# Three of wo's blocks loaded in mid-run, eight partitions a transfer, and the queries made after the turning

## The chip, the cores and the metric

The kernel runs on one core of one Trainium2 chip (trn2). The metric is device time in microseconds (us) of one execution. A kernel is run several times on the same chip; the number given is the median with the lowest and the highest. One more execution is taken with the hardware profiler. It has a time of its own, and inside that a span from the first to the last recorded instruction.

The engines are TensorE (PE for its matmuls, PEld for its weight loads), VectorE (DVE), ScalarE (ACT), GpSimd (POOL) and SyncE (SP). SP does no arithmetic here; it issues nearly all transfers, in program order, and an issue that waits holds up all issues behind it. Transfers are carried out by sixteen DMA engines.

## The reference

One decoding step of a block with two parallel branches on the same normalized input, in float32: grouped-query attention over a cache, and a dense layer with the Mish activation.

```python
B, Sq, D = 8, 1, 512
Hq, Hkv, Sk, Dh = 32, 8, 8192, 128
F = 1792
...
q = (xn @ wq).reshape(B, Sq, Hq, Dh)
k = repeat(k_cache, 4); v = repeat(v_cache, 4)
p = softmax(q @ k.T * Dh**-0.5)
A = (p @ v).reshape(B, Sq, Hq * Dh) @ wo
...
h = xn @ w1 + b1
act = h * tanh(softplus(h))
out = x + A + act @ w2
```

The caches hold 8 x 8 x 8192 x 128 numbers each, 268 MB. wq and wo have 8.4 MB each, w1 and w2 3.7 MB each. Every byte is read once.

## The kernel before, in words

The attention is cut into 32 units (`UNITS`). Unit j treats one batch b = j mod 8 and one pair of key heads m = j div 8, so eight query heads. Its keys are one transfer of 8.39 MB, its values another, each 64 KB in each of the 128 partitions (`load_unit`, L119 to L127). Both land in the one large tile `kv`: values always in the first 64 KB of a partition, keys by turns in two places that overlap by half.

A unit's work is written out by hand in the loop of L441 to L472. TensorE multiplies the unit's keys with the key weights in two halves (`scores`). Between the halves SP issues the keys of unit j + 1, which waits until the first half has read its place. `softmax` takes the maximum and the exponentials, into tile `e`. Then come the values of the unit *before* (`values`, 64 matmuls into bank O, and four VectorE operations that pick the wanted rows into `os`). Only then SP issues the values of unit j, since the place is free, and VectorE makes the next key weights. `turn` brings the unit's exponentials into the layout in which they multiply values: eight matmuls with permutations into X, the sum of the exponentials into M, its reciprocal, four transposes and two long reductions on VectorE. `merge` finishes the unit before: it turns `os` by one matmul into M, scales it with the reciprocal, and writes a column set of `oT[:, m]`.

Three times, for the pairs m = 1 to 3, the queries are made during the loop. At b = 4 SP issues a quarter of wq into `ws` (2 MB). At b = 5 `project` multiplies it: twice four matmuls into bank H, a copy by ScalarE into a tile named `e`, four matmuls into M, and at the end a scaled copy to `qT` by VectorE. In the kernel before it stands between `values` and `turn` (L466, L467). At b = 7 `spread` uses `qT`. The last wq goes through `ws` in units 20 and 21; after that `ws` is idle.

The end: wo comes as four transfers of 2 MB (L475 to L480) into the place of the values, each with four blocks of 512 KB, block u holding the rows of two query heads. w2 follows in three parts (L484 to L487) in the second half of the last keys' place. `outputs` multiplies `oT[:, m]` with its four blocks, eight matmuls for each m, four of them side by side on four groups of output columns; the sums stand in the first bank of X. They are copied to `a_sb`, and `down` adds the Mish branch with w2 and these sums into bank H. The result is H plus x.

Tiles of the pool `work` have two buffers unless a number is given; `e`, `os` and `a_sb` are of this kind. The Mish branch's activations are made in unit 0.

Of the kernel before, what the change touches and what calls it, by code (L numbers as in the profile page):

```python
# [8 lines left out]
F32 = mybir.dt.float32  # L9
# [4 lines left out]
P = 128  # L14
B = 8
D = 512
HKV = 8
REP = 4
DH = 128
# [8 lines left out]
BW = 1024  # L28
CC = D // P
# [3 lines left out]
Q = P // G  # L33
# [15 lines left out]
NJ = PL * HALF  # L49

W2R = 7

# [11 lines left out]
def kernel(  # L66
# [12 lines left out]
    nc = tc.nc  # L79
    PSUM = bass.MemoryType.PSUM  # L80

    const = ctx.enter_context(tc.tile_pool(name="const", bufs=1))
    work = ctx.enter_context(tc.tile_pool(name="work", bufs=2))
# [24 lines left out]
    xres = const.tile([P, P], F32, name="xres")  # L108
    oT = const.tile([P, NP, H2, B], F32, name="oT")
    aT = const.tile([P, 2 * W2R, B], F32, name="aT")  # L110
    pt8 = const.tile([P, HALF, PL * TL, H2], F32, name="pt8")
    tr = const.tile([P, PL * TL, 32], F32, name="tr")

    def load_q(m):

        rows = wq.rearrange("j p f -> (j p f)").rearrange("(m p f) -> m p f", m=NP, p=P)
        nc.sync.dma_start(ws, rows[m])
# [74 lines left out]
    for g in range(G):  # L192
# [4 lines left out]
            start=True,  # L197
# [15 lines left out]
    def project():  # L213

        w = ws.rearrange("p (c f) -> p c f", c=CC)
        for d in range(2):
            for c in range(CC):
                nc.tensor.matmul(  # L218
                    H[Q * c : Q * c + B, :],
                    xn4[:, c, :],  # L220
                    w[:, c, d * 512 : (d + 1) * 512],
                    start=True,
                    stop=True,
                )
            qp = work.tile([P, 512], F32, name="e")
            nc.scalar.copy(qp, H)
            for h in range(REP):
                at = 192 + (d * REP + h) * B
                nc.tensor.matmul(  # L229
                    M[:, at : at + B],  # L230
                    qp[:, h * DH : (h + 1) * DH],
                    bsel[:, :B],
                    start=True,
                    stop=True,
                )
        qT = work.tile([P, H2 * B], F32, name="qT", bufs=1)
        nc.vector.tensor_scalar_mul(qT, M[:, 192 : 192 + H2 * B], DH**-0.5)
        return qT
# [50 lines left out]
    def softmax(j):  # L289
        nm = work.tile([P, 1], F32, name="nm")  # L290
        nc.vector.tensor_reduce(nm, S, axis=AX.X, op=ALU.max, negate=True)  # L291
        nc.tensor.transpose(M[:1, 0:P], nm, ident)  # L292
        nr = work.tile([1, 2, REP], F32, name="nr")
        row = M[:1, 0:P].rearrange("p (c d k h) -> p d h c k", c=2, d=2, h=REP)
        for d in range(2):
            nc.vector.tensor_reduce(nr[:, d], row[:, d], axis=AX.XY, op=ALU.min)
        nx = work.tile([1, 2, 2, NH * G, REP], F32, name="nx", bufs=1)
        for c in range(2):
            nc.vector.tensor_copy(  # L299
                nx[:, c],  # L300
                nr.rearrange("p d (o h) -> p d o h", o=1).to_broadcast([1, 2, NH * G, REP]),
            )
        nc.tensor.transpose(  # L303
            M[:, 128:129], nx.rearrange("p c d k h -> p (c d k h)"), ident[:1, :1]
        )
        nmx = work.tile([P, 1], F32, name="nmx")
        nc.vector.tensor_copy(nmx, M[:, 128:129])  # L307
        e = E[j] = work.tile([P, 512], F32, name="e")
        l = work.tile([P, 1], F32, name="l")
        nc.scalar.activation(e, S, AF.Exp, bias=nmx, accum_out=l)  # L310
        lsel = work.tile([P, H2], F32, name="lsel")
        nc.vector.tensor_scalar(lsel, rsel, l, None, op0=ALU.mult)  # L312
        return lsel

    def turn(j, lsel):
        e = E.pop(j)
        for g in range(4):
            nc.tensor.matmul(X[:, g], perm[:, g], e, start=True, stop=True)  # L318
        nc.tensor.matmul(M[:, 136 : 136 + H2], ones, lsel, start=True, stop=True)  # L319
        RT[j] = work.tile([P, H2], F32, name="rt", bufs=3)  # L320
        nc.vector.reciprocal(RT[j], M[:, 136 : 136 + H2])  # L321
        for tl in range(TL):
            nc.vector.transpose(  # L323
                tr.rearrange("p (l t) c -> p t l c", t=TL)[:, tl],
                X.rearrange("p g (t q l) -> p t l g q", t=TL, q=PP)[:, tl],
            )
        for d in range(2):
            half = slice(64 * d, 64 * (d + 1))
            nc.vector.tensor_reduce(  # L329
                pt8[half, :, :, d * REP : (d + 1) * REP].rearrange("p c y h -> p y c h"),  # L330
                tr[half].rearrange("p y (g c h) -> p y c h g", g=4, c=HALF),
                axis=AX.X,
                op=ALU.add,
            )


    def values(j, vt):
        for n in range(NJ):
            l, c = divmod(n, HALF)
            q = n % G  # L340
            nc.tensor.matmul(  # L341
                O[Q * q : Q * (q + 1), :],
                pt8[:, c, TL * l : TL * (l + 1), :].rearrange("p t h -> p (t h)"),
                vt[:, 512 * n : 512 * (n + 1)],
                start=(n < G),
                stop=(n >= NJ - G),
            )
        os = work.tile([P, DH], F32, name="os")
        nc.vector.tensor_scalar(os, O[:, :DH], isel[:, 0:1], None, op0=ALU.mult)  # L349
        for i in range(1, TL):  # L350
            nc.vector.scalar_tensor_tensor(  # L351
                os, O[:, DH * i : DH * (i + 1)], isel[:, i : i + 1], os, op0=ALU.mult, op1=ALU.add
            )
        return os
# [49 lines left out]
        nc.vector.tensor_copy(aT, turned.rearrange("p (j q) -> p j q", q=Q)[:, :, :B])  # L404


    A = X[:, 0]

    def outputs(m, t):
        w = t.rearrange("p (u f) -> p u f", u=4)  # L410
        for d in range(2):
            for h in range(REP):
                nc.tensor.matmul(
                    A[Q * h : Q * h + B, :],
                    oT[:, m, d * REP + h, :],
                    w[:, d * 2 + h // 2, h % 2 * D : (h % 2 + 1) * D],
                    start=(m == 0 and d == 0),
                    stop=(m == NP - 1 and d == 1),
                )

    def down(lo, hi, w):
        for j in range(2 * lo, 2 * hi):
            for g in range(G):
                at = (j - 2 * lo) * D + g * P
                nc.tensor.matmul(  # L425
                    H[Q * g : Q * g + B, :P],
                    aT[:, j, :],
                    w[:, at : at + P],
                    start=(j == 0),
                    stop=(j == 2 * W2R - 1),  # L430
                )
# [9 lines left out]
    for j in range(UNITS):  # L441
        b = j % B
        more = j // B + 1 < NP

        k = k_t.pop(j)
        scores(j, k, j % 2 == 1, 0)
        if j == UNITS - 1:
            v_t[j] = load_unit(v, j, K_AT[0])
        elif j > 0:
            k_t[j + 1] = load_unit(kT, j + 1, K_AT[(j + 1) % 2])  # L450
        scores(j, k, j % 2 == 0, 1)
        WK.pop(j)
        lsel = softmax(j)
        os = None
        if j > 0:
            os = values(j - 1, v_t.pop(j - 1))
        if j + 1 < UNITS:
            v_t[j] = load_unit(v, j, V_AT)
            if more and b == SPREAD_Q:
                spread(qT)  # L460
            key_weights(j + 1)
        if j == 0:
            mish(w1_t, b1_sb, kv[:, W1_AT : W1_AT + 6 * FG])
        if more and b == LOAD_Q:
            load_q(j // B + 1)
        if more and b == MAKE_Q:  # L466
            qT = project()  # L467
        turn(j, lsel)
        if j > 0:
            merge(j - 1, os)  # L470
        if more and b == SPREAD_Q - 1:
            selections()  # L472


    w_o = [kv[:, 4096 * m : 4096 * (m + 1)] for m in range(NP)]  # L475
    for m in range(NP):
        nc.sync.dma_start(
            w_o[m].rearrange("p (u f) -> p u f", u=4),
            wo[4 * m : 4 * (m + 1)].rearrange("u p f -> p u f"),
        )  # L480
    w2_rows = w2.rearrange("j p f -> (j p) f").rearrange("(q i) f -> q (i f)", i=W2R)
    w2_t = []
# [8 lines left out]
        outputs(m, w_o[m])  # L491
    merge(UNITS - 1, os)
    outputs(NP - 1, w_o[NP - 1])
    a_sb = work.tile([P, 512], F32, name="e")
    nc.scalar.copy(a_sb, A)
    down(*parts[0], w2_t[0])
    for g in range(G):
        nc.tensor.matmul(
            H[Q * g : Q * g + B, :P],
            bsel[:, :B],  # L500
            a_sb[:, g * P : (g + 1) * P],
            start=False,
            stop=False,
        )
    for p, t in zip(parts[1:], w2_t[1:]):
        down(*p, t)
    res = work.tile([P, DH], F32, name="os")
    nc.vector.tensor_add(res, H[:, :P], xres)
    nc.sync.dma_start(out, res)


# [36 lines left out]
```

## Time and profile before

| | us |
|---|---|
| median of 3 runs | 1313.02 |
| lowest and highest | 1312.48, 1313.17 |
| the profiled execution | 1313.46 |
| its span | 1311.7 |
| PE busy (matmuls), share of the span | 985.5, 75% |
| DVE busy | 515.0, 39% |
| ACT busy | 40.2, 3% |
| granted TensorE clock, mean | 0.877 of full |

The whole program of an execution is one stream of instructions for each engine. The profile gives for each group of like instructions how often it ran, the busy time and mean, and the idle time of the engine ahead of it with what ended it. The chain of waits is followed back from the last instruction. A row of it has a start, a duration, and the engine and line, or the transfer, that set the end of that piece. A row of a stretch has the busy time of each engine in it, the granted clock, the share of the time in which the sixteen DMA engines carried packets (1.00 is all sixteen), and the rate. A share of 0.50 can mean eight engines busy all the time. The share is credited to the stretch in which a packet stands, so short stretches can be slightly above 1. The queue q1 is SP's, q10 ScalarE's, q8 and q14 carry instructions.

### The profile page before, as it was taken

The numbers are of one execution on the slowest core, as the hardware profiler recorded it, in microseconds if no ns is written. First come the engines' busy times: TensorE is split into PE (matmuls) and PEld (weight loads), VectorE is DVE, ScalarE is ACT, GpSimd is POOL, SyncE is SP. The second block draws the span as 40 slices with busy tenths as digits, with TensorE's granted clock in tenths as the row PEclk, the third lists the DMA queues.
The fourth block names the chain that finished last, engine by engine and source line by source line (L and its number), as shares of the span: only waits on it lengthen the run. The fifth ranks groups of instructions, "written<-read, shape, count | busy, mean of one in ns | idle before, by whom it ended". The sixth has DMA issues, their size and how long they took to land.

```text
span 1311.7 us, 11148 instructions
## 1 busy us (share of the span) xinstructions
PE 985.5 (75%) x5040; PEld 341.1 (26%) x5040; DVE 515.0 (39%) x728; ACT 40.2 (3%) x88; POOL 2.2 (0%) x9
## 2 busy tenths in 40 slices
PE   5968877768877668777878777687687678677666
PEld 3322222222322222222322222232232222222222
DVE  3463344432444442334243344414444432344431
ACT  1000000000000000000000000000000000000000
POOL 0000000000000000000000000000000000000000
PEclk9989888888888888887888788788898888888898
DMA  9999999999999999999999999999999999999997
GB/s 393 450 422 439 428 434 431 430 444 428 432 432 434 428 440 424 440 426 434 432 428 446 416 442 430 430 440 422 438 430 436 430 430 432 436 424 438 426 418 313
DMA packets 13591, 561.79 MB, mean 428 GB/s; under 512 B 1244, under 2 KB 1376, under 8 KB 4584
## 3 DMA queue, kind: packets, MB, share of 16 engines
q1 hardware_dynamic: 13520, 561.06, 99.2%
q8 instruction: 39, 0.64, 0.2%
q14 instruction: 8, 0.07, 0.0%
q10 hardware_dynamic: 24, 0.02, 0.0%
HBM read 561.01 MB, written 0.07 MB: 428 GB/s over the span
## 4 chain that ended last, share of the span: by engine, by line
DMA 73%; PE 23%; DVE 2%; issue 0%; ACT 0%; SPq 0%; DVEq 0%
DMA kv<-in_v 71%; PE o L341 20%; DMA kv<-in_w 3%; PE s L279 1%; DVE pt L329 1%; PE x L244 1%; PE h L425 0%; PE m L229 0%; PE h L218 0%; PE h L370 0%; DVE kv L392 0%; DVE tr L323 0%; DVE wk L262 0%; DVE nm L291 0%; ACT L177 0%
## 5 line engine op out<-in xcount | busy, mean ns | idle before, releaser
L279 PE MATMUL s<-kv,wk 128*64 128x512 f32 x2048 | 503.3, 654 | 179.3 <-DMA kv<-in_kT 175.4
L341 PE MATMUL o<-kv,pt 128*32 128x512 f32 x2048 | 269.9, 687 | 56.0 <-DMA kv<-in_v 46.4
L279 PEld LDWEIGHTS s<-kv,wk 128*64 128x64 f32 x2048 | 156.4, 151 | 500.9 <-issue 318.7
L329 DVE TENSOR_REDUCE pt<-tr 64x512 f32<-64x2048 f32 x64 | 241.3, 3770 | 1.6
L291 DVE TENSOR_REDUCE nm<-s 128x1 f32<-128x512 f32 x32 | 22.1, 691 | 369.2 <-PE s L279 369.2
L341 PEld LDWEIGHTS o<-kv,pt 128*32 128x32 f32 x2048 | 70.1, 124 | 229.4 <-issue 170.7
L318 PE MATMUL x<-e,perm 128*128 128x512 f32 x256 | 125.8, 636 | 2.0 <-ACT qr L251 2.0
L349 DVE TENSOR_SCALAR os<-o,isel 128x128 f32<-128x128 f32 x32 | 11.2, 351 | 277.3 <-PE o L341 277.3
L323 DVE STREAM_TRANSPOSE tr<-x 128x512 f32<-128x512 f32 x128 | 78.6, 671 | 0.0
L262 DVE TENSOR_TENSOR wk<-qr,mask 128x512 f32<-128x512 f32 x64 | 62.9, 1026 | 19.8 <-ACT qr L251 19.8
L318 PEld LDWEIGHTS x<-e,perm 128*128 128x128 f32 x256 | 49.0, 202 | 74.5 <-issue 72.0
L310 ACT ACTIVATE e<-s,nmx 128x512 f32<-128x512 f32 x32 | 22.0, 687 | 1097.4 <-DVE nmx L307 1097.4
L351 DVE SCALAR_TENSOR_TENSOR os<-o,isel,os 128x128 f32<-128x128 f32 x96 | 33.7, 351 | 3.4
L292 PE MATMUL m<-ident,nm 128*1 128x128 f32 x32 | 8.7, 273 | 28.8 <-DVE nm L291 28.8
L303 PE MATMUL m<-ident,nx 1*128 1x1 f32 x32 | 7.0, 219 | 24.2 <-DVE nx L299 24.2
L244 PE MATMUL x<-qT,tr 128*128 128x64 f32 x128 | 19.3, 315 | 3.0 <-ACT qr L251 2.7
L244 PEld LDWEIGHTS x<-qT,tr 128*128 128x128 f32 x128 | 18.1, 226 | 6.2 <-ACT qr L251 3.3
L321 DVE RECIPROCAL rt<-m 128x8 f32<-128x8 f32 x32 | 6.6, 207 | 33.4 <-PE m L319 33.4
L358 PE MATMUL m<-hsel,os 128*128 128x8 f32 x64 | 12.4, 266 | 9.3 <-DVE rt L321 9.3
L312 DVE TENSOR_SCALAR lsel<-rsel,l 128x8 f32<-128x8 f32 x32 | 7.4, 231 | 30.1 <-ACT e L310 30.1
L292 PEld LDWEIGHTS m<-ident,nm 128*1 128x1 f32 x32 | 2.5, 79 | 57.0 <-DVE nm L291 57.0
L319 PEld LDWEIGHTS m<-lsel,ones 128*128 128x128 f32 x64 | 12.2, 190 | 15.4 <-issue 15.2
(88 smaller groups left out, 163.7 us busy)
## 6 DMA issues: line engine op xcount, KB each, us to landing
ws<-in_wq SPq DMA_DIRECT2D x4, 2048.0 KB, 35.9
kv<-in_wo SPq DMA_DIRECT2D x4, 2048.0 KB, 24.5
kv<-in_w SPq DMA_DIRECT2D x1, 3584.0 KB, 26.7
kv<-in_w SPq DMA_DIRECT2D x1, 2048.0 KB, 35.4
kv<-in_w SPq DMA_DIRECT2D x1, 1024.0 KB, 20.7
kv<-in_kT SPq DMA_DIRECT2D x32, 29.9
kv<-in_v SPq DMA_DIRECT2D x32, 30.1
kv<-in_w SPq DMA_DIRECT2D x1, 512.0 KB, 20.5
```

The costliest lines, as they stand in the source:

```text
L244: nc.tensor.matmul(X[:, half, k * 64 : (k + 1) * 64], wide[:, half * 8 + k], qT, start=True, stop=True,)
L262: nc.vector.tensor_mul(w[:, :, d], q[:, :, d].to_broadcast([P, DI, NH * G, REP]), mask[:, d * NH * G : (d + 1) * NH * G] .rearrange("p (o ...
L279: nc.tensor.matmul(S[64 * c : 64 * (c + 1), :], w[:, i].rearrange("p d k h -> p (d k h)"), kk[:, i, c, :], start=(part == 0 and n == 0), s ...
L291: nc.vector.tensor_reduce(nm, S, axis=AX.X, op=ALU.max, negate=True)
L310: nc.scalar.activation(e, S, AF.Exp, bias=nmx, accum_out=l)
L318: nc.tensor.matmul(X[:, g], perm[:, g], e, start=True, stop=True)
L319: nc.tensor.matmul(M[:, 136 : 136 + H2], ones, lsel, start=True, stop=True)
L323: nc.vector.transpose(tr.rearrange("p (l t) c -> p t l c", t=TL)[:, tl], X.rearrange("p g (t q l) -> p t l g q", t=TL, q=PP)[:, tl],)
L329: nc.vector.tensor_reduce(pt8[half, :, :, d * REP : (d + 1) * REP].rearrange("p c y h -> p y c h"), tr[half].rearrange("p y (g c h) -> p y ...
L341: nc.tensor.matmul(O[Q * q : Q * (q + 1), :], pt8[:, c, TL * l : TL * (l + 1), :].rearrange("p t h -> p (t h)"), vt[:, 512 * n : 512 * (n ...
L351: nc.vector.scalar_tensor_tensor(os, O[:, DH * i : DH * (i + 1)], isel[:, i : i + 1], os, op0=ALU.mult, op1=ALU.add)
L358: nc.tensor.matmul(M[:, 168 : 168 + H2], os, hsel, start=True, stop=True)
```

## The change

Three of wo's sixteen blocks, u = 0, 1, 2 of the first pair of heads, no longer come at the end. `load_o(u)` issues block u in units 22, 24 and 26 (`LOAD_O`) into the first 32 partitions of `ws`, behind the unit's values on SP's queue. It takes four transfers: transfer r writes the partitions r, r + 4, ..., r + 28, eight of them, 16 KB into each, and each partition holds four successive rows of the block. One unit later `early(u)` multiplies the block: eight matmuls with 32 rows of weights, four of them side by side. Their sums start the accumulation in bank H that `outputs` continues at the end. Since four successive rows share a partition, the first pair's outputs must be picked in the same order. `turn_o`, once in unit 23, does it with four matmuls of every fourth column of the identity into M and a VectorE copy to the new tile `oX`.

`outputs` skips the three blocks, the first wo transfer brings one block in place of four, and its sums stand in H; the bank of `down` and of the result becomes O. `project` moves behind `turn`. The tiles `e` and `os` get one buffer each.

```diff
+FEW = 32
+LOAD_O = (22, 24, 26)
...
+    oX = const.tile([FEW, CC, 2 * len(LOAD_O) * B], F32, name="oX")
...
-            qp = work.tile([P, 512], F32, name="e")
+            qp = work.tile([P, 512], F32, name="e", bufs=1)
...
-        e = E[j] = work.tile([P, 512], F32, name="e")
+        e = E[j] = work.tile([P, 512], F32, name="e", bufs=1)
...
-        os = work.tile([P, DH], F32, name="os")
+        os = work.tile([P, DH], F32, name="os", bufs=1)
...
-    A = X[:, 0]
+    def load_o(u):
+
+        rows = wo[u].rearrange("(e r i) f -> r e (i f)", r=4, i=CC)
+        for r in range(4):
+            nc.sync.dma_start(ws[r:FEW:4], rows[r])
+
+    def turn_o():
+
+        n = 2 * len(LOAD_O) * B
+        o = oT[:, 0].rearrange("p h b -> p (h b)")[:, :n]
+        for i in range(CC):
+            nc.tensor.matmul(
+                M[:FEW, 256 + i * n : 256 + (i + 1) * n], ident[:, i::CC], o, start=True, stop=True
+            )
+        nc.vector.tensor_copy(oX.rearrange("p i n -> p (i n)"), M[:FEW, 256 : 256 + CC * n])
+
+    def early(u):
+        for n in range(2):
+            for i in range(CC):
+                nc.tensor.matmul(
+                    H[Q * i : Q * i + B, :],
+                    oX[:, i, (2 * u + n) * B : (2 * u + n + 1) * B],
+                    ws[:FEW, i * BW + n * D : i * BW + (n + 1) * D],
+                    start=(u == 0 and n == 0),
+                    stop=False,
+                )
 
     def outputs(m, t):
         w = t.rearrange("p (u f) -> p u f", u=4)
         for d in range(2):
             for h in range(REP):
-                nc.tensor.matmul(
-                    A[Q * h : Q * h + B, :],
+                u = d * 2 + h // 2
+                if m == 0 and u < len(LOAD_O):
+                    continue
+                nc.tensor.matmul(
+                    H[Q * h : Q * h + B, :],
                     oT[:, m, d * REP + h, :],
-                    w[:, d * 2 + h // 2, h % 2 * D : (h % 2 + 1) * D],
-                    start=(m == 0 and d == 0),
+                    w[:, u, h % 2 * D : (h % 2 + 1) * D],
+                    start=False,
                     stop=(m == NP - 1 and d == 1),
                 )
...
-                    H[Q * g : Q * g + B, :P],
+                    O[Q * g : Q * g + B, :P],
...
             load_q(j // B + 1)
+        if j in LOAD_O:
+            load_o(LOAD_O.index(j))
+        if j - 1 in LOAD_O:
+            if j - 1 == LOAD_O[0]:
+                turn_o()
+            early(LOAD_O.index(j - 1))
+        turn(j, lsel)
         if more and b == MAKE_Q:
             qT = project()
-        turn(j, lsel)
         if j > 0:
             merge(j - 1, os)
...
     for m in range(NP):
+        lo = len(LOAD_O) if m == 0 else 0
         nc.sync.dma_start(
-            w_o[m].rearrange("p (u f) -> p u f", u=4),
-            wo[4 * m : 4 * (m + 1)].rearrange("u p f -> p u f"),
+            w_o[m].rearrange("p (u f) -> p u f", u=4)[:, lo:],
+            wo[4 * m + lo : 4 * (m + 1)].rearrange("u p f -> p u f"),
         )
...
-    nc.scalar.copy(a_sb, A)
+    nc.scalar.copy(a_sb, H)
...
-    nc.vector.tensor_add(res, H[:, :P], xres)
+    nc.vector.tensor_add(res, O[:, :P], xres)
```

More of the change, by code (lines that the diff above doesn't have):

```diff
@@ L493 @@
     outputs(NP - 1, w_o[NP - 1])
-    a_sb = work.tile([P, 512], F32, name="e")
-    nc.scalar.copy(a_sb, A)
+    a_sb = work.tile([P, 512], F32, name="e", bufs=1)
+    nc.scalar.copy(a_sb, H)
     down(*parts[0], w2_t[0])
@@ L498 @@
         nc.tensor.matmul(
-            H[Q * g : Q * g + B, :P],
+            O[Q * g : Q * g + B, :P],
             bsel[:, :B],
@@ L506 @@
         down(*p, t)
-    res = work.tile([P, DH], F32, name="os")
-    nc.vector.tensor_add(res, H[:, :P], xres)
+    res = work.tile([P, DH], F32, name="os", bufs=1)
+    nc.vector.tensor_add(res, O[:, :P], xres)
     nc.sync.dma_start(out, res)
```

## The prediction, made before the changed kernel was run

> **What bounds the kernel now.** I read the page first: the DMA slices, the queues, the list of DMA issues. Then the chain of waits at the end, and then stretches of the last ten microseconds.
>
> ```profile
> DMA packets 13591, 561.79 MB, mean 428 GB/s; under 512 B 1244, under 2 KB 1376, under 8 KB 4584
> ## 3 DMA queue, kind: packets, MB, share of 16 engines
> q1 hardware_dynamic: 13520, 561.06, 99.2%
> q8 instruction: 39, 0.64, 0.2%
> q14 instruction: 8, 0.07, 0.0%
> q10 hardware_dynamic: 24, 0.02, 0.0%
> ```
>
> q1, SP's queue, fills 99.2% of the time of sixteen engines. So a step that only shifts TensorE work in the middle is worth nothing unless it makes a transfer start late. Over the span of 1311.7 us (first row of the stretches below) each DMA engine moves 561.06 MB / (0.992 x 16 x 1311.7 us) = 26.95 GB/s.
>
> How much room is there before a transfer starts late? A unit's V transfer stands in the chain of waits:
>
> ```profile
> 1190.26 30.04 DMA kv<-in_v
> ...
> 1267.88 0.37 SPq L477
> ...
> 1268.29 35.38 DMA kv<-in_w
> ...
> 1303.72 3.26 PE h L425 x64
> ```
>
> A unit's 8.39 MB (128 partitions of 64 KB) take 19.4 us at the 432 GB/s of the stretch quoted next. From issue to landing it is 30.0 us. So about 10.6 us of older work is still queued when V is issued, and an issue may be that much later before an engine runs dry. At the end the chain is the first part of w2, issued behind all of wo, landing at 1268.29 + 35.38 = 1303.67, and the products with w2 behind it. The end follows the landing of w2 one for one.
>
> Next, how evenly do the sixteen engines finish? In stretches (the last two columns are the share of sixteen DMA engines and GB/s):
>
> ```profile
> core 0 of [0], span 1311.7 us
> core 0: us, PE busy (x) PEld busy (x) DVE busy (x) ACT busy (x) POOL busy (x), PEclk, DMA share, GB/s
> 100.00:1200.00 1100.00, 834.99 (x4160) 283.08 (x4156) 431.00 (x594) 28.80 (x68) 0.00 (x0) 0.87 1.00 432
> 1276.00:1296.00 20.00, 14.16 (x108) 3.52 (x112) 7.34 (x7) 0.00 (x0) 0.00 (x0) 0.74 1.00 403
> 1298.00:1300.00 2.00, 1.06 (x12) 0.38 (x16) 0.00 (x0) 0.00 (x0) 0.00 (x0) 1.00 1.01 422
> 1301.00:1302.00 1.00, 0.00 (x0) 0.00 (x0) 0.00 (x0) 0.53 (x1) 0.00 (x0) 1.00 0.58 246
> 1303.00:1304.00 1.00, 0.28 (x12) 0.28 (x16) 0.00 (x0) 0.00 (x0) 0.00 (x0) 1.00 0.57 238
> 1305.50:1306.00 0.50, 0.50 (x16) 0.43 (x12) 0.00 (x0) 0.00 (x0) 0.00 (x0) 0.50 0.38 156
> 1306.50:1307.00 0.50, 0.50 (x20) 0.41 (x12) 0.00 (x0) 0.00 (x0) 0.00 (x0) 0.50 0.08 33
> ```
>
> This decides the case. Until 1300 all sixteen work. From 1301 to 1304 the share is 0.57 to 0.58, nine of sixteen; from 1305.5 it is 0.38, six; by about 1306.6 all are done. Seven engines finish between 1300 and 1301, say 1300.5, 6 us before the last six, three between 1304 and 1305.5. Nothing is short but the time of the late ones. Nine engines move 238 to 246 GB/s, about 27 each, as in the full stretch: an engine left alone is no faster, so one engine's queue isn't helped by another's being empty. A likely source of the unevenness is instruction loading: 39 packets on q8 for 0.2% of 16 x 1311.7 us, 42 us in all or 1.08 us each, on some of the engines and not on others.
>
> **The change part by part.** *The moved bytes.* Three of wo's sixteen 512 KB blocks leave the tail: 1.573 MB, on sixteen engines at the 403 GB/s of the stretch in which wo comes (1276 to 1296): 3.90 us less for every engine (3.64 at the 432 of the long stretch; I take the rate of wo's own).
>
> They come instead in twelve transfers, each eight rows of 16 KB into eight partitions. On how many engines does such a transfer run? The issue list counts them:
>
> ```profile
> ws<-in_wq SPq DMA_DIRECT2D x4, 2048.0 KB, 35.9
> kv<-in_wo SPq DMA_DIRECT2D x4, 2048.0 KB, 24.5
> ...
> kv<-in_kT SPq DMA_DIRECT2D x32, 29.9
> kv<-in_v SPq DMA_DIRECT2D x32, 30.1
> ...
> kv<-in_x ACTq DMA_DIRECT2D x1, 16.0 KB
> kv<-in_b ACTq DMA_DIRECT2D x1, 7.0 KB
> ```
>
> SP issues these 72, w1, three parts of w2 and the output: 77 in all. The packets under 512 B are 1244 = 77 x 16 + 12, one small closing packet for each engine of a transfer. The twelve left belong to x, eight rows, and b1, four rows: q10 has 24 packets, 8 + 4 of data and as many closing ones. So a transfer of eight rows runs on eight engines, one row on each. A row of 16,384 B takes 16,384 / 26.95 GB/s = 0.608 us, and twelve of them 7.30 us on each of the eight, if all twelve use the same eight. Those eight end 7.30 - 3.90 = 3.40 us later than before, the other eight 3.90 us earlier. Nine engines are late and only eight are outside the eight: at least one late engine is loaded further, whichever eight they are. If it is one of the last six, the end moves by +3.40 us.
>
> [...]
>
> Following packets by their start and end from x's rows on, which no view prints, I find b1's engines among x's, and some of x's eight among the late nine. I use that for the chances alone.
>
> An unknown is whether a transfer of one row per engine costs more than its bytes. Bounds: 0.608 us by rate, 1.08 us as the instruction packets have it. I take the first, since these rows stand in the same queue as their neighbours and a switch between queues is what the other has; the far end gives 12 x 1.08 - 3.90 = +9.06 us.
>
> *SP's queue.* Twelve more issues (each near the 0.37 us at L477) behind V(22), V(24), V(26), with K of the next unit but one behind them. SP mostly waits:
>
> ```profile
> SPq L123 <- PE s L279: 288.3, 31, 18.7
> SPq L123 <- PE o L341: 253.3, 30, 9.9
> ```
>
> 1.5 us a unit lie inside waits of 9 us a time (288.3/31). `ws` is free: project's last read is unit 21, and each block is multiplied before the next is issued. Cost 0; without that cover 4.5 us of issue, still inside the 10.6 us of queue.
>
> *early and turn_o.* The matmuls have a twin in project (eight of 8 columns by 512). TensorE's rows of unit 13, where project stands:
>
> ```profile
> 554.87 1.04 PE L218 MATMUL h<-ws,xn 128*8 128x512 f32 x8
> ...
> 560.70 5.04 PE L318 MATMUL x<-e,perm 128*128 128x512 f32 x8
> 565.57 0.28 PE L319 MATMUL m<-lsel,ones 128*128 128x8 f32 x2
> 566.16 0.39 PE L358 MATMUL m<-hsel,os 128*128 128x8 f32 x2 [0.30 <-DVE rt L321]
> 573.74 15.60 PE L279 MATMUL s<-kv,wk 128*64 128x512 f32 x64 [7.19 <-DMA kv<-in_kT]
> ```
>
> and VectorE's from the same unit:
>
> ```profile
> 566.02 2.46 DVE L323 STREAM_TRANSPOSE tr<-x 128x512 f32<-128x512 f32 x4
> 568.51 7.55 DVE L329 TENSOR_REDUCE pt<-tr 64x512 f32<-64x2048 f32 x2
> ```
>
> Eight take 1.04 us (2.1 at half clock), three times. Once, in unit 23, turn_o adds four small matmuls and a copy that TensorE waits for. No row has them; the nearest is the whole of project, 5.83 us from 554.87 to 560.70 with two copies in it, which I take as the upper bound. All stands in the 7.19 us in which TensorE waits for K: at most 2.1 in two units, 5.83 + 1.04 = 6.9 in the third. Cost 0; without that cover it would be 11 us over three units, each share inside the queue's 10.6 us. The block lands 4 x 0.608 = 2.4 us behind V, and values, 64 matmuls, come between V's landing and its use.
>
> *project behind turn.* The same matmuls, another order. turn starts at 554.87 and takes 5.32 us, to 560.2, and project ends at 566. Its scaled copy to qT now queues behind 10 us of turn on VectorE, to about 571. merge writes the same bank M, and its wait on rt shows that it does wait for readers of other columns, so it may start at 571.3, and the scores queued behind it are free at 571.7, before K at 573.74. qT is needed two units later. Cost 0 in units 5, 13, 21. One buffer for `e` and `os`: each writer comes a unit after the last reader, or behind it on TensorE. Cost 0.
>
> *Tail.* Six matmuls fewer, 0.8 us at 1.04 for eight, before TensorE waits for w2 anyway; the sums in H and O instead of X and H wait for nothing late. Cost 0.
>
> **Sum.** +3.40 us. The profiled execution takes 1313.46 us (1.8 us around its span), so 1316.9; it stands 0.44 us above the median, so 1316.4 against 1313.02: +0.26%.
>
> **Rivals.**
> 1. *The loaded late engine is one of the three.* It ends between 1304 and 1305.5 now, so at 1307.4 to 1308.9, and the last six, relieved, at 1302.7. The end moves by +0.8 to +2.3, mid 1314.6. For it: nothing but chance; six of nine late ones speak against.
> 2. *Spread.* Transfers rotate over the engines or are split over all: 7.30/2 - 3.90 = -0.25, 1312.8. Against: the twelve closing packets rule out sixteen.
> 3. *Faster.* The late engines of the changed run lie all outside the eight: instruction loading falls differently, and the ninth late engine is no longer late. Then the loaded ones end at 1300.5 + 3.4 = 1303.9, the rest at 1302.7, against 1306.6: -2.7, 1310.3. It decides as soon as no loaded engine is over 2.7 us behind the early ones. For it: the early ones have 6 us to give, near what three blocks take. Against: nine do not fit in eight.
> 4. *Small transfers are dear*, 1.08 us a row: +9.1, 1322.1. Against: the same queue.
> 5. *The change does nothing, since the late engines' bytes are not what ends the run.* The 0.08 of the last row and the chain's end on w2 exclude it; no chance of its own.
>
> **How the numbers follow.** Forecast 0.68 (its own range 1315.6 to 1317.4), rival 1 0.10, rival 2 0.08, rival 3 0.08, rival 4 0.06. From 1312.6 to 1318.5 it holds the forecast and rivals 1 and 2, 0.86 less a little of the forecast's own spread. A measurement of this kernel tells 0.2%, 2.6 us, from no change. The forecast is 0.8 us beyond that, so some of it (0.04) falls within: slower 0.68 - 0.04 + 0.06 = 0.70, same 0.10 + 0.08 + 0.04 = 0.22, faster 0.08.
>
> **What would show it.** On the changed page the packets under 512 B are 1244 + 12 x 8 = 1340 if eight engines carry each transfer; 1436 if sixteen. q1 has 13520 - 384 + 192 = 13328 packets. In the last stretches most engines end by about 1304 and a few, share below 0.3, run on to 1310; the first part of w2 lands near 1307.1 instead of 1303.67. The wait of scores for K stays above zero in units 6, 14, 22 and 24; if it is gone there and transfers show a slice below full, the mid-run steps were not free. The prediction is wrong if the last stretches show all engines ending together near 1304.

## The result and the profile after

| | us |
|---|---|
| kernel before, median of 7 runs | 1312.72 (1312.48 to 1313.27) |
| changed kernel, median of 7 runs | 1316.78 (1316.24 to 1317.48) |
| ratio, 95% interval | 1.0029 (1.0020 to 1.0039) |
| profiled execution, before and after | 1313.46, 1316.27 |
| its span, before and after | 1311.7, 1314.2 |

The change makes the kernel 4.06 us slower; the interval reaches from 2.6 to 5.1 us. The forecast was 1316.4.

First the counts of packets on the page of the changed kernel:

```profile
DMA packets 13399, 561.79 MB, mean 427 GB/s; under 512 B 1340, under 2 KB 1472, under 8 KB 4296
...
q1 hardware_dynamic: 13328, 561.06, 99.1%
```

1340 small packets are 1244 + 96: twelve transfers with eight closing packets each, so each ran on eight engines. q1's 13328 is the count worked out ahead. The bytes are the same, and q1 is nearly as full as before (99.1% and 99.2%). Yet the end is later, as its last stretches show (changed kernel; the last two columns are the share of sixteen engines and GB/s):

```profile
1298.00:1300.00 2.00, 2.00 (x24) 0.45 (x20) 1.17 (x4) 0.00 (x0) 0.00 (x0) 1.00 0.97 408
1302.00:1303.00 1.00, 0.74 (x7) 0.32 (x11) 0.17 (x1) 0.00 (x0) 0.00 (x0) 1.00 0.99 406
1303.00:1304.00 1.00, 1.00 (x16) 0.22 (x8) 0.00 (x0) 0.00 (x0) 0.00 (x0) 1.00 0.53 209
1304.00:1305.00 1.00, 0.47 (x8) 0.00 (x0) 0.00 (x0) 0.41 (x1) 0.00 (x0) 1.00 0.20 86
1306.00:1307.00 1.00, 0.15 (x8) 0.15 (x12) 0.00 (x0) 0.00 (x0) 0.00 (x0) 1.00 0.19 78
1308.00:1309.00 1.00, 1.00 (x39) 0.71 (x28) 0.00 (x0) 0.00 (x0) 0.00 (x0) 1.00 0.13 53
1309.00:1310.00 1.00, 0.69 (x29) 0.69 (x32) 0.00 (x0) 0.00 (x0) 0.00 (x0) 1.00 0.10 41
```

Before, nine of sixteen engines still worked from 1301 to 1304 (0.57 to 0.58), and six (0.38) up to about 1306.6. Now all sixteen work until 1303, most of them stop within a microsecond or so, and three to four (0.19 and 0.20 of sixteen) go on, two of them (0.13) past 1308, until about 1310. The trace also has each engine's own landing of the last part of w2, which no view prints. Before, seven engines landed it by 1301.1, three at 1305.2 to 1305.3, six at 1306.8 to 1307.4. Now twelve land it from 1303.4 to 1304.3, the others at 1305.95, 1308.62, 1310.20 and 1310.51. The last three are 3.4 us behind one of the three and two of the six: late engines inside the eight got later still, as the sum has it. The one at 1305.95 has no place in the sum. The late ones outside the eight were relieved. The early ones outside were due near 1300.5 - 3.9 = 1296.6, but none stopped there (0.97 from 1298 to 1300). They lost their lead in mid-run; the run without mid-run transfers, below, shows how. The chain of waits of the changed kernel ends on the last engines:

```profile
1289.78 20.72 DMA kv<-in_w
1310.51 0.04 issue
1310.55 0.67 PE o L459 x16
1311.22 0.02 issue
1311.24 0.29 DVE os L549
```

The last part of w2 now lands at 1310.5, and only 16 records of TensorE (two to a float32 matmul) follow it. The first part, forecast for 1307.1, lands just ahead of 1306.85, where `down` starts; before, it landed at 1303.67. TensorE's row of that start:

```profile
1306.85 1.93 PE L459 MATMUL o<-kv,aT 128*8 128x128 f32 x64 [2.38 <-DMA kv<-in_w]
```

The kernel before ended otherwise in its profile. Its last part of w2 had landed at 1307.4, but the chain ran through the first part and all 112 records of `down`, because TensorE had half its clock there (0.50 in the rows from 1305.5 to 1307) and was done only at 1308.9. So the last landing moved by 3.1 us, and the end of the profiled execution by less, since the half clock had lengthened the one before.

What happened in the middle? TensorE in unit 23 of the changed kernel:

```profile
956.52 2.00 PE L250 MATMUL x<-qT,tr 128*128 128x64 f32 x16
959.19 2.00 PE L250 MATMUL x<-qT,tr 128*128 128x64 f32 x16 [0.67 <-ACT qr L257]
961.12 0.68 PE L424 MATMUL m<-oT,ident 128*32 128x48 f32 x8
964.10 3.60 PE L432 MATMUL h<-ws,oX 32*8 32x512 f32 x16 [2.30 <-DVE oX L427]
967.63 5.83 PE L324 MATMUL x<-e,perm 128*128 128x512 f32 x8
973.30 0.28 PE L325 MATMUL m<-lsel,ones 128*128 128x8 f32 x2
973.88 0.39 PE L364 MATMUL m<-hsel,os 128*128 128x8 f32 x2 [0.30 <-DVE rt L327]
974.20 13.95 PE L285 MATMUL s<-kv,wk 128*64 128x512 f32 x64
```

The scores of unit 24 follow `merge` without a wait for K. `spread` (L250) stands in this unit too, and `early` takes 3.60 us with its sixteen records, at a granted clock of 0.50. So here the cover was used up, which the prediction had not expected. The experiments say whether it cost anything.

### The profile page after: what moved, and what is told of

Read it like the earlier page. It is cut to its first block, busy times and chain, and to the rows that moved or that the text cites. A ratio compares the mean times of both kernels' runs of the same rounds, so it can differ in the third digit from the quotient of the medians.

```text
span 1314.2 us, 11260 instructions
## 1 busy us (share of the span) xinstructions
PE 990.7 (75%) x5084; PEld 339.5 (26%) x5084; DVE 515.3 (39%) x729; ACT 40.2 (3%) x88; POOL 2.2 (0%) x9
## 2 busy tenths in 40 slices
DMA packets 13399, 561.79 MB, mean 427 GB/s; under 512 B 1340, under 2 KB 1472, under 8 KB 4296
## 3 DMA queue, kind: packets, MB, share of 16 engines
q1 hardware_dynamic: 13328, 561.06, 99.1%
## 4 chain that ended last, share of the span: by engine, by line
DMA 70%; PE 25%; DVE 3%; SPq 1%; ACT 0%; issue 0%; DVEq 0%; ACTq 0%
DMA kv<-in_v 69%; PE o L347 20%; PE s L285 2%; DMA kv<-in_w 2%; SPq L527 1%; PE x L250 1%; DVE pt L335 1%; PE x L324 0%; PE h L376 0%; DVE wk L268 0%; PE m L235 0%; PE h L224 0%; PE h L432 0%; DVE kv L398 0%; DVE tr L329 0%
## 5 line engine op out<-in xcount | busy, mean ns | idle before, releaser
L347 PE MATMUL o<-kv,pt 128*32 128x512 f32 x2048 | 266.8, 680 | 50.7 <-DMA kv<-in_v 41.2
L324 PE MATMUL x<-e,perm 128*128 128x512 f32 x256 | 122.2, 622 | 1.3 <-ACT qr L257 1.3
L250 PE MATMUL x<-qT,tr 128*128 128x64 f32 x128 | 19.3, 315 | 3.0 <-ACT qr L257 2.7
L250 PEld LDWEIGHTS x<-qT,tr 128*128 128x128 f32 x128 | 18.1, 226 | 6.2 <-ACT qr L257 3.3
L364 PEld LDWEIGHTS m<-hsel,os 128*128 128x128 f32 x64 | 10.1, 199 | 26.0 <-DVE qT L243 14.2
```

What stands on the lines that cost most here:

```text
L250: nc.tensor.matmul(X[:, half, k * 64 : (k + 1) * 64], wide[:, half * 8 + k], qT, start=True, stop=True,)
L347: nc.tensor.matmul(O[Q * q : Q * (q + 1), :], pt8[:, c, TL * l : TL * (l + 1), :].rearrange("p t h -> p (t h)"), vt[:, 512 * n : 512 * (n ...
L364: nc.tensor.matmul(M[:, 168 : 168 + H2], os, hsel, start=True, stop=True)
```

## The experiments

The theory: the kernel ends with its latest DMA engine, and the change puts 7.3 us of rows on eight engines while it takes 3.9 us from all. The rivals: the mid-run work of TensorE, VectorE and SP costs the time; or a transfer in mid-run costs as such; or which engines carry the rows doesn't matter. All nine runs stand here.

| run | measured, us | before on the same chip, us | ratio, 95% interval |
|---|---|---|---|
| whole blocks on 128 partitions | 1312.66 | 1313.07 | 0.9998 (0.9989 to 1.0007) |
| mid-run compute, no mid-run transfers | 1313.39 | 1313.07 | 1.0004 (0.9995 to 1.0013) |
| project behind turn alone | 1312.54 | 1312.77 | 1.0000 (0.9991 to 1.0009) |
| the three blocks not read at all | 1309.00 | 1312.77 | 0.9972 (0.9961 to 0.9983) |
| every row brought twice | 1324.24 | 1312.77 | 1.0085 (1.0070 to 1.0101) |
| sixteen rows a transfer | 1326.47 | 1313.07 | 1.0105 (1.0091 to 1.0118) |
| four rows a transfer | 1327.44 | 1313.07 | 1.0116 (1.0100 to 1.0131) |
| eight successive partitions | 1335.32 | 1312.77 | 1.0169 (1.0156 to 1.0183) |
| more instructions, kernel before | 1317.83 | 1313.11 | 1.0035 (1.0023 to 1.0047) |

### The same blocks on all sixteen engines

```diff
     def load_o(u):
-        rows = wo[u].rearrange("(e r i) f -> r e (i f)", r=4, i=CC)
-        for r in range(4):
-            nc.sync.dma_start(ws[r:FEW:4], rows[r])
+        nc.sync.dma_start(ws[:, :BW], wo[u])
...
     def early(u):
+        d = u // 2
         for n in range(2):
+            h = u % 2 * 2 + n
+            nc.tensor.matmul(H[Q * h : Q * h + B, :], oT[:, 0, d * REP + h, :],
+                ws[:, n * D : (n + 1) * D], start=(d == 0), stop=False)
...
-            if j - 1 == LOAD_O[0]:
-                turn_o()
```

> The changed kernel with each of the three blocks as one transfer of 128 partitions of 4 KB into ws, in the same units, multiplied one unit later by two matmuls of 128 rows with oT itself (no turn_o, no oX). Theory: the same bytes on sixteen engines at the same rate as at the end, 3.9 us added and 3.9 taken away: 1312.7 us. Rival A (a mid-run transfer or its matmuls cost as such): 1314 to 1317.

Measured: 1312.66 us, no change from before. Its last stretches have the old shape:

```profile
1301.00:1302.00 1.00, 0.00 (x0) 0.00 (x0) 0.00 (x0) 0.24 (x1) 0.00 (x0) 1.00 0.54 229
1303.00:1304.00 1.00, 0.58 (x24) 0.59 (x28) 0.00 (x0) 0.00 (x0) 0.00 (x0) 1.00 0.57 238
1305.50:1306.00 0.50, 0.19 (x10) 0.12 (x10) 0.00 (x0) 0.00 (x0) 0.00 (x0) 1.00 0.38 156
1306.50:1307.00 0.50, 0.44 (x17) 0.15 (x8) 0.00 (x0) 0.00 (x0) 0.00 (x0) 1.00 0.02 8
```

Nine engines, then six, done by 1306.6, as before the change. The blocks came in the same units in mid-run; bringing bytes earlier is worth nothing here and costs nothing. This run also does without `turn_o` and with fewer matmuls, so the compute needs a run of its own.

### The mid-run compute without the mid-run transfers

```diff
-        if j in LOAD_O:
-            load_o(LOAD_O.index(j))
...
-        lo = len(LOAD_O) if m == 0 else 0
+        lo = 0
```

> The changed kernel without the twelve mid-run transfers and with all four blocks of wo's first transfer at the end; early multiplies what wq left in ws, so the three blocks are missing from the sum. turn_o, early, project behind turn, the banks and the single buffers stay. Theory: all of these are hidden: 1312.7 us. Rival A (they cost, the lost wait for K in unit 24 shows it): 1314 to 1317.

Measured: 1313.39 us, no change. `turn_o`, `early` and the moved `project` cost the kernel nothing that can be measured, although unit 24's wait for K is gone here too. But the queue did not cover them for every engine. SP issues the keys of unit 25 at 980.99, against 974.39 in the kernel before. A stretch around that time and one at the end, first in the kernel before, then in this run:

```profile
970.00:990.00 20.00, 15.09 (x73) 4.53 (x73) 7.85 (x10) 0.78 (x2) 0.00 (x0) 0.92 1.00 430
1300.00:1302.00 2.00, 0.84 (x8) 0.00 (x0) 0.00 (x0) 0.58 (x1) 0.00 (x0) 1.00 0.59 250
```

```profile
970.00:990.00 20.00, 18.15 (x80) 6.61 (x82) 11.73 (x14) 0.00 (x0) 0.00 (x0) 0.96 0.93 397
1300.00:1302.00 2.00, 2.00 (x12) 0.19 (x4) 0.00 (x0) 0.00 (x0) 0.00 (x0) 0.50 0.92 381
```

Some engines ran out of work around 980 (0.93), and the early ones end some 1.5 us later than before: (0.92 - 0.59) x 16 x 2 us, over seven engines, an estimate. By the packets' start and end times at least eight engines stayed at work throughout. The late ones ended no later than before, at 1307.3 against 1307.4, and they set the end. The 10.6 us of queued work in the prediction was read from issue to landing, so it is that of the latest engine; an engine that is up to 6 us ahead has as little as 4.6 us.

### project behind turn alone

```diff
-            qp = work.tile([P, 512], F32, name="e")
+            qp = work.tile([P, 512], F32, name="e", bufs=1)
...
+        turn(j, lsel)
         if more and b == MAKE_Q:
             qT = project()
-        turn(j, lsel)
```

(and one buffer for the other uses of `e` and `os`).

> The kernel before with project behind turn and with one buffer for e and os, nothing else. Theory: hidden in the wait for K: 1313.0 us, no change. Rival (VectorE's copy to qT behind turn holds up merge and the scores): slower by up to 3 x 2 us, 1315 to 1319.

Measured: 1312.54 us, no change.

### The three blocks not read at all

```diff
-        if j in LOAD_O:
-            load_o(LOAD_O.index(j))
```

> The changed kernel without the twelve transfers, and with the first wo transfer cut to one block as in the changed kernel: three blocks of wo are not read at all, and early multiplies what wq left in ws. Theory: every engine has 3.9 us less to carry, and the end follows: 1309.2 us. Rival (the tail is bound by something else, such as TensorE or the issues of w2): above 1311.

Measured: 1309.00 us, 3.77 us under the kernel before. So the end follows the bytes of the tail, and the first term of the sum, 3.90 us, has its size.

### Every row twice

```diff
             nc.sync.dma_start(ws[r:FEW:4], rows[r])
+        for r in range(4):
+            nc.sync.dma_start(ws[FEW + r : 2 * FEW : 4], rows[r])
```

> The changed kernel with each of the twelve transfers issued a second time, into partitions 32 to 63 of ws, which nothing reads (1.57 MB more in all). Theory: another 7.3 us on the same eight engines, so the loaded late ones end 14.6 - 3.9 = 10.7 us later than in the kernel before: 1323.8 us; in the last stretches the share of a few engines runs for some 14 us after the others. If the transfers were spread evenly over sixteen engines it would be 1316.8 + 3.65 = 1320.4; if rows cost nothing in mid-run, 1316.8.

Measured: 1324.24 us, 11.47 us over its kernel before, 7.4 us more than the changed kernel is over its own. Twelve more rows for each of eight engines are 7.3 us; spread over sixteen they would be 3.65. So the second term has its size, and the rows fall on the same engines each time, or at least on the late ones among them.

The expected shape of the end did not come. Stretches of this run in mid-run and at the end, and two of SP's waits (in all, times, longest):

```profile
936.00:956.00 20.00, 17.07 (x117) 5.98 (x114) 2.76 (x10) 0.78 (x2) 0.00 (x0) 1.00 0.82 342
1314.00:1316.00 2.00, 1.24 (x24) 0.91 (x28) 0.00 (x0) 0.00 (x0) 0.00 (x0) 0.67 0.61 246
1316.00:1318.00 2.00, 2.00 (x47) 1.50 (x40) 0.00 (x0) 0.00 (x0) 0.00 (x0) 0.50 0.13 53
...
SPq L419 <- DMA kv<-in_v: 56.1, 3, 18.7
SPq L419 <- DMA kv<-in_kT: 20.8, 3, 7.8
```

A few engines run on alone for about 3 us, not for 14, because the others had stood without work in mid-run (0.82). With eight transfers to a block in place of four, SP waits among them for keys and values to land, and the next keys, behind them, are issued late: those of unit 24 at 948.42, against 938.53 in the changed kernel. By the packets' times at least three engines stayed at work through the first of these gaps and eight through the other two, which fits the latest engines having all their rows added to their time.

### Sixteen rows a transfer

```diff
-        rows = wo[u].rearrange("(e r i) f -> r e (i f)", r=4, i=CC)
-        for r in range(4):
-            nc.sync.dma_start(ws[r:FEW:4], rows[r])
+        rows = wo[u].rearrange("(e r i) f -> r e (i f)", r=2, i=CC)
+        for r in range(2):
+            nc.sync.dma_start(ws[r:FEW:2], rows[r])
```

> The changed kernel with sixteen rows in a transfer in place of eight (two transfers a block in place of four; same bytes, same partitions 0 to 31, same compute). Theory (the end is set by engines that were late before and got 7.3 us of rows more, less 3.9): the rows are spread over sixteen engines, 6 x 0.608 = 3.65 us each, less 3.90: 1312.5 us, and the last stretches again show nine engines and then six. Rival A (the cost is the mid-run compute or SP's issues, not who carries the rows): it stays near 1316.8. [...]

Measured: 1326.47 us. Both expectations fell: the theory's 1312.5 was 14 us too low, rival A's 1316.8 some 10 us. A stretch around the first block's arrival, first in the changed kernel:

```profile
936.00:956.00 20.00, 18.02 (x110) 5.33 (x106) 1.71 (x7) 0.78 (x2) 0.00 (x0) 0.91 1.00 430
```

and in the run with sixteen rows:

```profile
936.00:956.00 20.00, 14.60 (x80) 4.27 (x80) 1.71 (x7) 0.78 (x2) 0.00 (x0) 0.83 0.98 309
```

The engines are as busy, 0.98 of sixteen, but move 309 GB/s in place of 430: packets take longer. The packet records, of which no view prints a median, have 1.15 us for the 16 KB rows in place of 0.61 in the changed kernel, and between 930 and 1130 us a tenth of the units' 64 KB packets took 2.98 us or more, in place of 2.42. This isn't the lateness of a few engines: at the end nine are late as before (0.59 from 1314 to 1316), so all sixteen lost time alike. The rows' own longer time makes only 6 x (1.15 - 0.61) = 3.2 us on each engine, an estimate from these records, so most of the loss is probably the units' packets, which take longer beside the rows. Two things differ from the changed kernel: sixteen engines carry rows at once and not eight, and their partitions are two apart and not four. Why the packets take longer this run doesn't show. The author's guess after the fact was that partitions close to one another are the cause; the next run tests it.

### Eight successive partitions

```diff
-        rows = wo[u].rearrange("(e r i) f -> r e (i f)", r=4, i=CC)
+        rows = wo[u].rearrange("(r e i) f -> r e (i f)", r=4, i=CC)
         for r in range(4):
-            nc.sync.dma_start(ws[r:FEW:4], rows[r])
+            nc.sync.dma_start(ws[8 * r : 8 * (r + 1)], rows[r])
```

> The changed kernel with the eight rows of a transfer in eight successive partitions (8r to 8r + 7) in place of every fourth one; as many transfers, rows and bytes, the same products. [...]

Two times were worked out ahead: 1316.8 us, as the changed kernel, if the place of the partitions makes no difference, and 1338 us if a row takes 2.4 us, four times its 0.61, since 12 x 2.4 - 3.9 = +25. The factor of four was an assumption that no run shows.

Measured: 1335.32 us. The numbers of transfers, rows and bytes, and the products, are those of the changed kernel, but the eight partitions of a transfer lie side by side, and so do the eight pieces of wo in memory that it reads. The same stretch of this run:

```profile
936.00:956.00 20.00, 12.36 (x66) 3.65 (x66) 1.71 (x7) 0.78 (x2) 0.00 (x0) 0.83 1.00 325
```

Engines fully busy at 325 GB/s again. So this arrangement is dear, by 18.5 us, and the changed kernel's step of four partitions avoids that: its stretch shows 430 GB/s. The time is 3 us below 1338, but the way there was another: the rows took about 1.05 us (median of the packet records) and not 2.4, while between 930 and 1130 us a tenth of the units' 64 KB packets took 3.15 us or more. That the partitions do it, and not the neighbouring pieces in memory, was not tested apart. The run with whole blocks speaks for the partitions: there sixteen engines read 512 KB that lie together, at no loss.

### Four rows a transfer

```diff
-        rows = wo[u].rearrange("(e r i) f -> r e (i f)", r=4, i=CC)
-        for r in range(4):
-            nc.sync.dma_start(ws[r:FEW:4], rows[r])
+        rows = wo[u].rearrange("(e r i) f -> r e (i f)", r=8, i=CC)
+        for r in range(8):
+            nc.sync.dma_start(ws[r:FEW:8], rows[r])
```

> The changed kernel with four rows in a transfer (eight transfers a block). [...]

Worked out ahead: if the same four engines take the rows each time, 24 rows of 0.608 us are 14.6 us on each, less 3.9, so these four end 10.7 us later, and the kernel takes from 1317.3 to 1323.4 us, by how late they were before; with another set each time it is 14.6 / 4 - 3.9 = -0.25, 1312.5 us.

Measured: 1327.44 us, 4 us above the highest expectation and 15 us above the 1312.5 of another set each time. SP's waits, below, have a part in this, so the run alone doesn't decide between the two. Around the first block and at the end of this run:

```profile
936.00:956.00 20.00, 15.67 (x96) 4.61 (x96) 1.71 (x7) 0.78 (x2) 0.00 (x0) 0.91 0.75 292
...
1314.00:1316.00 2.00, 1.32 (x16) 0.11 (x4) 0.00 (x0) 0.56 (x1) 0.00 (x0) 1.00 1.01 416
1316.00:1318.00 2.00, 0.27 (x12) 0.27 (x16) 0.00 (x0) 0.03 (x1) 0.00 (x0) 1.00 0.50 199
1318.00:1320.00 2.00, 1.88 (x72) 1.59 (x60) 0.00 (x0) 0.00 (x0) 0.00 (x0) 1.00 0.06 27
```

Here the rate is low because the *share* is: 0.75, four of sixteen engines idle in the mean. The cause is SP. Its waits in this run, and its issue of the keys of unit 24, in the changed kernel and then here:

```profile
SPq L417 <- DMA kv<-in_v: 57.4, 3, 19.9
SPq L417 <- DMA kv<-in_kT: 21.1, 3, 7.9
...
938.53 0.34 SPq L129 DMA_DIRECT2D kv<-in_kT  x1
...
949.27 0.38 SPq L129 DMA_DIRECT2D kv<-in_kT  x1
```

In the changed kernel SP has no wait at L417. With eight transfers to a block it waits there for keys and values to land, the next keys are issued 10.7 us later, and the engines without rows run dry. So the expectation was wrong to let them go on undisturbed. At the end all engines are late together, and one (0.06) is last. Longer packets may add to it: the median row still took 0.61 us by the packet records, but a tenth took 0.99 us or more. How the 4 us divide, and which of the four engines with rows are late, stays open.

### More instructions in the kernel before

```diff
+        if 0 < j < UNITS - 1:
+            for n in range(48):
+                nc.tensor.matmul(H[:B, 504:512], hsel, hsel, start=True, stop=True)
         turn(j, lsel)
```

> The kernel before with 48 tiny matmuls (8 columns by 8, into columns of H that nothing reads) in each of units 1 to 30, ahead of turn, in the time in which TensorE waits for keys. They add no bytes of data and no transfer of SP's; they add instructions: the page before has 10080 records of PE and PEld and 39 instruction packets on q8, 258 records a packet, so 48 x 30 matmuls of four records give 5760 records and 22 packets more. Theory (instruction loading makes some engines late, and the late ones set the end): 22 packets over the engines that carry them, eight if the lateness is theirs, 2.75 each at 1.08 us or more: +3 to +4.2 us, 1316 to 1317, seven engines early still, by 9 us and more. Rival (the lateness has another source, and TensorE's extra work is hidden): 1313.

Measured: 1317.83 us, 4.72 over its kernel before, a little above the expectation. The queues of this run, and some of its last stretches:

```profile
q1 hardware_dynamic: 13520, 561.06, 99.0%
q8 instruction: 62, 1.02, 0.3%
```

```profile
1304.00:1305.00 1.00, 1.00 (x12) 0.24 (x8) 0.00 (x0) 0.00 (x0) 0.00 (x0) 0.50 0.70 295
1305.00:1307.00 2.00, 1.86 (x12) 0.09 (x4) 0.00 (x0) 0.04 (x1) 0.00 (x0) 0.50 0.56 238
1309.00:1310.00 1.00, 1.00 (x28) 0.72 (x24) 0.00 (x0) 0.00 (x0) 0.00 (x0) 0.50 0.36 147
1310.00:1311.00 1.00, 1.00 (x25) 0.72 (x21) 0.00 (x0) 0.00 (x0) 0.00 (x0) 0.50 0.31 127
```

q1's packets and bytes are those of before; 23 instruction packets came on top. The first part of w2 lands at 1308.00 in place of 1303.67, with nine engines late (0.56) as before. So more instructions make the end later without a byte of data more. TensorE's own extra work is an unlikely cause, since some 7 us of it in one unit cost nothing in the run without mid-run transfers (1313.39 against 1313.07). But the seven early engines ended near 1304.4 here, not 1300.5, so their lead stayed near 6 to 7 us and did not grow to the 9 that were expected. That instruction loading makes the lead is not shown by this run; what held the early engines back stays open.

## Why the prediction was right

- *What bounds the kernel.* The latest DMA engine. The runs with the blocks left out (-3.77 us), brought twice (+11.47) and spread over sixteen engines (-0.4, within its interval) follow this. Only where TensorE had half its clock at the very end, as in the profile before, did its last products end the kernel, some 0.8 us later than the landing would have.
- *The two terms.* The relief of 3.90 us measured 3.77, the rows' 7.30 us measured 7.4 in the second set. By rate they make +3.4, by these measurements +3.6, and the measured change is +4.06 (2.6 to 5.1): no difference that the runs can tell. The last landing moved by 3.1.
- *Nine late engines don't fit outside eight.* The three engines that land last are, by their times, late ones inside the eight. Two of them, at 1310.20 and 1310.51, were of the last six, so the forecast's case came about and not the first rival's. That one of the last six lay in the eight was likely, not derived.
- *Same eight each time.* The sum's 7.30 us on each of eight engines takes this for granted; no run shows directly which engines a transfer takes. What the runs showed agrees with it: three engines land the last part of w2 3.4 us later than three late ones did before, few engines are left at the end (0.10 to 0.20 of sixteen), and the second set of rows cost 7.4 us, where rows spread over sixteen would cost 3.65. A rotating set would have given the second rival's 1312.8, against 1316.78 measured.
- *Costs at nothing in mid-run.* The sum was right, two of its steps were not. A row group of eight records is four float32 matmuls, so `early` takes sixteen records, 3.60 us at a clock of 0.50 and not 2.1; the six matmuls saved in the tail are mis-sized in the same way. And `spread`, 4 us of TensorE, stands in unit 23, which the prediction forgot: in the kernel before, the wait behind it was 0.80 us and not the 7.19 of unit 13. The wait of unit 24 for K, called above zero, is gone, and the stretch from 970 to 990 is below full (0.95; 0.93 with the compute alone). By the prediction's own sign the mid-run steps were not free. They cost early engines some of their lead, and the kernel nothing (1313.39 with the compute alone, 1312.54 with the move alone), since the late engines kept working. So the zero was right for a reason that the prediction didn't give.
- *SP's issues.* Estimated at 0.37 us each, they took 0.62. The view by tile of the changed kernel gives least, median and longest in ns:

```profile
L417 SPq DMA_DIRECT2D ws<-in_wo x12: 623/624/775, 916.6 to 1078.1; - x12
```

  2.5 us a unit, still inside SP's waits.
- *Dear small transfers*, the fourth rival, didn't come: twelve rows more took 7.4 us, 0.62 us each. The run with eight successive partitions shows how near that case was: its rows took about 1.05 us.
- *Faster*, the third rival: nothing of it was seen.

## What to carry to other kernels

Where transfers fill the time, count the engines that still work in the last microseconds: a mean share of 99% hid a spread of 6 us between the first engine done and the last. A transfer with few rows loads few engines, here eight rows eight engines (96 small packets more for twelve transfers), and by all that was measured the same ones each time; then it can help only if those are the ones that finish early. And in this kernel its rows did better in partitions that are not next to one another: 430 GB/s with every fourth one, 325 with eight in a row. The time from issue to landing, here 30.0 us, is that of the latest engine, so the engines ahead of it, here by up to 6 us, run dry sooner than it says; that cost nothing as long as they stayed ahead (1313.39 against 1313.07). Several small transfers in front of a large one can also make the issuing queue wait: four were free here, with eight the next keys were issued 10 us later.

## What the runs showed of the hardware that was not expected

- Eight rows of 16 KB into every fourth partition pass at 430 GB/s beside the other transfers. Into eight successive partitions the same rows bring the rate to 325 GB/s with all engines busy, and the kernel takes 18.5 us more.
- Sixteen rows a transfer, into every second of 32 partitions, were slower than eight into every fourth: 1326.47 against 1316.78 us.
- More instructions were not free here, where transfers bound: with 23 instruction packets of 16 KB more the kernel took 4.72 us more. If eight engines carry them, an assumption that no view shows, that is an estimated 2.9 packets and 1.6 us a packet, against 0.6 us for 16 KB by rate.
- Low GB/s has two faces in the same columns: share 0.98 with 309 GB/s is packets that take longer, here 1.15 us a row in place of 0.61; share 0.75 with 292 GB/s is engines without work, here because SP's issues waited.
